# Sixth block pair of a SwiGLU layer in the 11-product Strassen form, with a new order for all engines

## The chip, the cores and the metric

One core of one Trainium2 chip runs the kernel. The metric is the device time of one execution in microseconds (us). Three runs of the kernel before took 2497.64, 2503.82 and 2503.84 us, median 2503.82. The engines are called as the profile calls them: PE is TensorE (PEld its weight load), DVE VectorE, ACT ScalarE, POOL GpSimd, SP the engine that issues most DMAs. Each engine works through its own queue in order and waits on semaphores of the others.

## What is computed

`x` is (8, 4096, 192). Two layers follow each other:

```python
# light convolution: 8 heads of 24 channels, 7 taps, softmax over the taps
w = softmax(weight, axis=-1)
out = einsum('hk,bskhg->bshg', w, windows_of(x_pad, 7))
# SwiGLU feed-forward on the 32768 tokens, d_model 192, d_ff 1536
xn = x / sqrt(mean(x*x, -1) + 1e-6) * rms_g
g = xn @ w_gate
return (silu(g) * (xn @ w_val)) @ w_out
```

## The kernel before, in words

The 32768 tokens are cut into 32 *pairs* of 1024 tokens, a pair being two groups of 512. Pair 0 and the conversion of the weights form the start. Pair 1 is computed with plain f32 matmuls. Pairs 2 to 31 are all computed alike, one *window* of time each.

**Products.** d_ff is 1536 = 12 chunks of 128. Two chunks make a *block pair* j (0 to 5), which together with the two token groups is a 2 x 2 block product with the cells a, b, c, d. Each cell holds the gate (upper half of a PSUM bank pair) and the value (the other). One product of the window (`product`, matmul at L899) is 6 matmuls of 512 columns: three split parts (high, middle, low words of f32, in the type fp32r) by two row halves. In the *plain* form (0 in `FORM`) a block pair takes 12 products, named Aa to Ed. In the *Strassen* form (1) it takes 11, named P1 to P7 and Q1 to Q4, and the cells are put together with copies and sums between the products, which the table `ORDER` names f1, f3, f4 and f5:

```python
if act == "f1":                       # b's bank starts as a copy of a's
    self.open((j, "b"), True)
    copy(eng, self.both(j, "b"), self.both(j, "a"))
elif act == "f3":                     # c's products are put aside in SBUF (tt)
    copy(eng, s5, self.both(j, "c"))
elif act in ("f4", "f5"):             # c = b + s5, later d = b + s5
    c = "c" if act == "f4" else "d"
    ...
    nc.vector.tensor_tensor(out=self.both(j, c), in0=self.both(j, "b"), in1=s5, op=ALU.add)
```

The copies are at L667 (ACT) and L669 (DVE), the sums at L967 (DVE, 128x1024). There are four PSUM bank pairs in all. A cell takes one from its first product until it is evacuated: `g` is the Silu on ACT (L973), `m` the product with the value on DVE (L980), which writes the 128x512 hidden tile `ht` and gives the bank back.

**Out steps.** The second matmul (42 steps a window, `step`, L923, names o1.0 to o7.5) uses a Strassen form as well, with 7 products by 6 block pairs. Step o2.j, for instance, reads a cell that `h2` has overwritten in place, and `h1` to `h4` (`h_sum`, L950, on DVE or POOL) make these sums. h2.j overwrites the cell that step o1.j reads. Steps o1 and o7 open accumulators X and Z, each in a freed bank pair. At the end `c1`, `c2`, `s7` copy accumulators, `C22`, `C21` (L997) add them, `T11` to `T22` (L938) transpose them, and `st` stores them.

**The next pair's input.** While a window runs, other engines prepare the pairs that follow: seven taps of the convolution (`cv0` to `cv6`, L431 and L435, 128x1536), square, reduction, factor and scale (`sq`, `red`, `pow`, `bc`, `mul`), eight DMAs to a scratch tensor in DRAM (`pl`), six DMAs back in the other layout into tile `xb` (`ft`, L631), eight DMAs that load the input of the pair after that (`ld`, L146). Then four sums of token blocks (`x1` to `x4`, `x_sum`, L827; x2 needs x1, x4 needs x2) and the split in three words for each of five operands: `n` is a copy to fp32r (L667 ACT, L669 DVE), `l` and `d` are at L813 and L815.

**Weights.** The split pieces lie in DRAM and are streamed through a ring of 10 slots (`ring<-wd`, L785, 192 KB each, SP). Each freed slot starts the next load; a plain block pair has 6 pieces, a Strassen one 9.

**What sets the order.** Nothing is scheduled at build time: four tables are the order of work. `LINE` is PE's: 69 products and 42 out steps. `ORDER` is one window: each word is an engine letter (V = DVE, G = POOL, A = ACT, S = SP), an act and a block pair or part; `p3` stands for three steps of `LINE`, `-` means the pair before, `+` and `++` the next one and the one after. `FIRST` is the window of pair 1, where `W` is a step of the preparation of the split weights (`prepare`, L749 to L768). `prepare(o)` works on as regular a slice of block pairs as `FORM` allows:

```python
kind = {2: 1, 4: 1, 6: 1, 8: 1, 9: 0}.get(o)
mine = [j for j in range(NP) if kind in (None, FORM[j])]
step = {b - a for a, b in zip(mine, mine[1:])}
if len(step) > 1:
    return slice(0, NP)
```

In `ORDER` of before PE runs, from the window's start, 15 out steps of the pair before, one product, one out step, four products, three out steps, then 64 products without a break and 23 out steps; the long stretches of out steps of two windows join into one of 38.

Of the kernel before, what the change touches and what calls it, by code (L numbers as in the profile page):

```python
# [20 lines left out]
def kernel(  # L21
# [46 lines left out]
    SPAN = 1509  # L68
    SPLIT = 2.0**-12
    HIGH = 0xFFFFF000  # L70
    FORM = (1, 0, 1, 0, 1, 0)
    PLAIN = tuple((j, c) for j in range(NP) for c in "abcd")
    ORDER = (
        "Vd.0 An.4 An.3 Ac2- p5- Gh4.2- Vl.2 Vd.4 Vh4.3- Vl.3 Vd.3 Vl.0 Vd.2 Vh4.0- Vh4.5-",
        "p8- Gh4.4- Gh4.1- VT11- VC22- p2- p1 Gl.4 Acv0+ Af1.0 VT22- VC21- p1- VT21- p3 Vcv1+",
        "p1 Af3.0 Ast1.2- Vcv2+ Vf4.0 p3- p3 Aga.0 Ast1.0- Vcv3+ VT12- Vma.0 Sst0.2- Agc.0",
        "Ast0.3- p1 Vf5.0 p2 Vcv4+ p1 Vmc.0 Vcv5+ p2 Sst1.3- p1 Sst0.4- Sst0.0- Agb.0 Ast1.1-",
        "Agc.1 Ast0.1- Vmb.0 p2 Vcv6+ Agd.0 p2 Aga.1 Vmd.0 Vma.1 Vmc.1 p1 Asq+ Vred+ p1 Af1.2",
        "Sst1.4- Gh1.0 Agb.1 Vmb.1 p1 Gpow+ p3 Af3.2 p1 Vf4.2 p4 Aga.2 Agd.1 Vma.2 Vbc+ Vf5.2",
        "Gmul+ p1 Agc.2 p1 Apl.0+ Apl.1+ Apl.2+ p1 Vmd.1 Vmc.2 p6 Agd.2 Agb.2 Apl.3+ Vmb.2",  # L80
        "Vmd.2 Apl.4+ p1 Agb.3 Aga.3 Apl.5+ p1 Vmb.3 Vma.3 p4 Af1.4 Vf3.4 Agc.3 Apl.6+ Apl.7+",
        "p3 Vmc.3 p1 Vf4.4 p2 Aga.4 Gh1.1 p1 Agd.3 Aft.0+ Sft.2+ Vma.4 Vf5.4 Vh3.1 Sft.3+",
        "Aft.1+ Sld.0++ Vmd.3 Sft.4+ Sld.1++ Sft.5+ Sld.2++ Sld.3++ Sld.4++ Sld.5++ Sld.6++",
        "Sld.7++ p7 Gh1.3 Agc.4 Agd.4 Vmc.4 Vmd.4 Agb.4 p1 Vh1.2 Vh3.0 Vmb.4 p7 An.0+ p1",
        "Aga.5 Agd.5 p1 Vh1.4 An.1+ Vx1+ Vmd.5 Vma.5 p1 Gh3.3 p2 Gh3.2 Agb.5 p2 Gh3.4 p2 Gx3+",
        "Agc.5 Vd.1+ p1 Vh2.0 Vmc.5 Vh2.1 Vmb.5 Vh1.5 Vh2.2 Vh3.5 Vl.1+ Vh2.5 Vh2.4 Ac1 p1",
        "Gx2+ An.2+ p6 Gh2.3 Gx4+ As7 p8",
    )
    FIRST = (
        "p1 Vcv5+ W p2 Vcv6+ p1 Aga.0 Vma.0 p2 Asq+ W W p1 Agb.0 W Vmb.0 W p1 Vred+ p2 Agc.0",  # L90
        "Vmc.0 W p1 Gpow+ W W W p1 W p1 Agd.0 W Vmd.0 p1 Vbc+ Gh1.0 p1 Gmul+ p1 Aga.1 Vh3.0 W",
        "Vma.1 p1 W W W W p1 W p1 Agb.1 Apl.0+ Vmb.1 p1 Apl.1+ p1 Apl.2+ W p1 Agc.1 Apl.3+ W",
        "W W Vmc.1 Apl.4+ p1 W W Apl.5+ p1 Apl.6+ p1 Agd.1 Apl.7+ Vmd.1 p1 Gh1.1 W p1 W W W",
        "p1 Aga.2 Vh3.1 W Vma.2 W p3 Agb.2 Vmb.2 W p1 W W W p1 W p1 Agc.2 W Vmc.2 p3 Agd.2 W",
        "Vmd.2 p1 W W W Vh1.2 W p1 W p1 Aga.3 Gh3.2 Vma.3 p2 W p1 Agb.3 W W W Vmb.3 p1 W W p1",
        "Aft.0+ p1 Aft.1+ Agc.3 Sft.2+ Vmc.3 p1 Sft.3+ W p1 Sft.4+ W W W Sft.5+ p1 Agd.3 W",
        "Vmd.3 W p1 Gh1.3 p2 Aga.4 Gh3.3 Vma.4 W p1 W W p1 W p1 Agb.4 W Vmb.4 p3 Agc.4 W",
        "Vmc.4 p1 W p2 Agd.4 An.1+ Vmd.4 p1 Vx1+ Sld.0++ Vh1.4 p1 Gx3+ Vd.1+ p1 Aga.5 Gh3.4",
        "Vma.5 Vl.1+ Sld.1++ p1 Gx2+ p1 An.2+ p1 Agb.5 Sld.2++ Gx4+ Vmb.5 p1 Sld.3++ p2 Agc.5",
        "Sld.4++ Vmc.5 p1 Sld.5++ p1 Sld.6++ Agd.5 p1 An.0+ Vmd.5 p1 Vh2.0 Sld.7++ Vh1.5 p2",  # L100
        "Gh2.3 Vh3.5 Vh2.5 p1 Vh2.1 p1 Vh2.4 p1 Ac1 Vh2.2 p2 R p7 As7 p7",
    )
    LINE = (
        "P1.0 P5.0 P6.0 P2.0 Q1.0 P7.0 P3.0 Q2.0 Ac.1 Q4.0 Q3.0 P4.0 Bc.1 Ec.1 Aa.1 Ba.1 Ea.1",
        "Ab.1 Eb.1 P1.2 Bb.1 P5.2 P6.2 P2.2 Q1.2 Ad.1 Ed.1 P7.2 P3.2 Bd.1 Q2.2 Q3.2 Q4.2 Aa.3",
        "Ba.3 P4.2 Ea.3 Ab.3 Bb.3 Eb.3 Ac.3 Bc.3 P1.4 P5.4 Ec.3 P6.4 P2.4 Q1.4 Ad.3 Bd.3 P7.4",
        "Ed.3 Q2.4 P3.4 Q4.4 P4.4 Ad.5 Q3.4 Ed.5 Aa.5 Ea.5 Ab.5 Bd.5 Ac.5 Bc.5 Ba.5 Bb.5 Ec.5",
        "Eb.5 o1.0 o1.5 o1.3 o1.1 o1.4 o1.2 o7.0 o7.3 o7.4 o2.0 o7.1 o7.2 o2.5 o6.0 o7.5 o6.2",
        "o2.3 o6.1 o2.4 o6.4 o6.3 o6.5 o4.4 o2.1 o4.1 o5.0 o2.2 o5.5 o4.3 o5.3 o4.5 o5.2 o5.4",
        "o5.1 o4.2 o4.0 o3.5 o3.2 o3.3 o3.1 o3.4 o3.0",  # L110
    )

    cst = ctx.enter_context(tc.tile_pool(name="cst", bufs=1))
# [605 lines left out]
    def blocks(o):  # L719
# [4 lines that stand above are left out]
# [600 lines left out]
```

## Time and profile before

| | |
|---|---|
| three runs | 2497.64, 2503.82, 2503.84 us |
| the profiled execution | 2498.01 us, span 2496.2 us, granted PE clock 0.999 |
| PE busy | 2477.4 us, 29140 matmul records |
| DVE busy | 2013.4 us, 2482 instructions |
| ACT, POOL busy | 926.6 and 852.5 us |
| one window, 373.85 to 449.52 us | 75.67 us: PE 75.67, DVE 62.62, ACT 27.90, POOL 26.14 busy |
| window of pair 1, 129.04 to 222.66 us | 93.62 us: PE 93.62, DVE 67.77, ACT 36.72, POOL 43.72 busy |

Part 1 of the page gives busy time by engine, part 4 the chain of work that ended last (what each step on it waited for), part 5 the costliest groups of instructions by line. The trace also answers with the chain in order of time and with timelines of one engine, in which a bracket tells how long the engine sat idle before an instruction and what ended that.

### The profile page before, as it was taken

What the parts mean: (1) busy time and instruction counts of PE and PEld (TensorE: products, weight loads), DVE (VectorE), ACT (ScalarE), POOL (GpSimd) and SP (SyncE); (2) the same over time, 40 slices, a digit from 0 to 9 for tenths busy, and PEclk for the clock granted to TensorE, in tenths of its full rate; (3) what the DMA queues carried; (4) which work ended last, traced back from release to release, by engine and by line L of the source; (5) the groups of instructions that cost most, each with busy time, mean ns of one, the idle gap of its engine ahead of it and who ended that gap; (6) DMA issues with size and microseconds to landing.
All of it is one profiled execution on the core that took longest, in us unless ns stands there. A gap on an engine that the chain in (4) does not pass through costs nothing.

```text
span 2496.2 us, 69094 instructions
## 1 busy us (share of the span) xinstructions
PE 2477.4 (99%) x29140; PEld 1932.4 (77%) x29140; DVE 2013.4 (81%) x2482; ACT 926.6 (37%) x1349; POOL 852.5 (34%) x640
## 2 busy tenths in 40 slices
PE   8999999999999999999999999999999999999999
PEld 5647778877777787777877788777777877778887
DVE  8668888788878788878888788888787888888864
ACT  6443334333333333333333343333333333333331
POOL 0553333423243324343333333233433233333331
PEclk9999999999999999999999999999999999999999
DMA  7365667766678666677666677666686666786652
GB/s 150 59 189 152 155 170 192 173 180 157 156 171 205 169 166 158 160 180 193 172 160 157 168 192 176 179 154 157 170 201 172 165 158 162 181 197 171 159 140 81
DMA packets 701735, 412.22 MB, mean 165 GB/s; under 512 B 506610, under 2 KB 687730, under 8 KB 701426
## 3 DMA queue, kind: packets, MB, share of 16 engines
q1 hardware_dynamic: 540176, 353.65, 56.1%
q10 hardware_dynamic: 161250, 54.16, 9.7%
q8 instruction: 230, 3.77, 0.6%
q14 instruction: 79, 0.65, 0.1%
HBM read 349.26 MB, written 58.39 MB: 163 GB/s over the span
## 4 chain that ended last, share of the span: by engine, by line
PE 96%; DMA 2%; SPq 1%; DVE 0%; ACT 0%; issue 0%; ACTq 0%; DVEq 0%
PE ps L899 56%; PE ps L923 34%; PE ps L871 2%; PE ps L1070 2%; DMA xb<-xd 1%; PE ps L1111 1%; SPq L146 0%; SPq L229 0%; DMA ht<-in_moe_w_gate_dram 0%; DMA x<-in_x_dram 0%; DMA ht<-in_moe_w_val_dram 0%; ACT tt L973 0%; DVE ht L980 0%; SPq L631 0%; ACT o_sb L1119 0%
## 5 line engine op out<-in xcount | busy, mean ns | idle before, releaser
L899 PE MATMUL ps<-part,ring 64*128 64x512 f32 x12420 | 1442.9, 389 | 0.0
L899 PEld LDWEIGHTS ps<-part,ring 64*128 64x128 f32 x12420 | 1185.8, 184 | 236.5 <-issue 18.0
L973 ACT ACTIVATE tt<-ps 128x512 f32<-128x512 f32 x744 | 430.9, 598 | 726.4 <-PE ps L899 586.4
L980 DVE TENSOR_TENSOR ht<-ps,tt 128x512 f32<-128x512 f32 x744 | 495.5, 684 | 190.5 <-ACT tt L973 185.3
L923 PE MATMUL ps<-ht,wo_sb 128*32 128x384 f32 (+2 forms) x6696 | 443.1, 380 | 3.3 <-DVE ht L980 3.3
L923 PE MATMUL ps<-ht,x 128*32 128x256 f32 (+2 forms) x6696 | 441.9, 379 | 0.0
L950 POOL TENSOR_TENSOR ht<-ht 128x512 f32<-128x512 f32 x186 | 283.7, 1538 | 433.3 <-PE ps L923 377.1
L950 POOL TENSOR_TENSOR hs<-ht 128x512 f32<-128x512 f32 x93 | 120.2, 1293 | 834.2 <-DVE ht L980 832.3
L923 PEld LDWEIGHTS ps<-ht,wo_sb 128*32 128x32 f32 x6696 | 296.2, 110 | 121.9 <-issue 21.5
L923 PEld LDWEIGHTS ps<-ht,x 128*32 128x32 f32 x6696 | 302.5, 110 | 90.6
L435 DVE SCALAR_TENSOR_TENSOR y<-xh,tp,y 128x1536 f32<-128x1536 f32 x186 | 342.5, 1841 | 1.3
L667 ACT COPY ps<-ps 128x384 f32<-128x384 f32 (+1 forms) x121 | 104.1, 860 | 408.7 <-PE ps L899 311.7
L967 DVE TENSOR_TENSOR ps<-ps,tt 128x1024 f32<-128x1024 f32 x180 | 221.3, 1229 | 42.1 <-PE ps L899 35.0
L667 ACT COPY tt<-ps 128x384 f32<-128x384 f32 (+1 forms) x122 | 91.0, 746 | 227.0 <-PE ps L923 207.8
L923 PE MATMUL ps<-hs,x 128*32 128x128 f32 (+2 forms) x2232 | 161.0, 379 | 0.0
L950 DVE TENSOR_TENSOR ht<-ht 128x512 f32<-128x512 f32 x186 | 126.5, 693 | 8.0 <-POOL hs L950 4.6
L923 PEld LDWEIGHTS ps<-hs,x 128*32 128x32 f32 x2232 | 108.9, 110 | 27.7
L667 ACT CAST part<-xb 128x1024 fp32r<-128x1024 f32 x87 | 91.3, 1050 | 104.0 <-DMA xb<-xd 67.1
L950 DVE TENSOR_TENSOR ht<-hs,ht 128x512 f32<-128x512 f32 x155 | 122.4, 806 | 2.9 <-PE ps L923 1.1
L950 DVE TENSOR_TENSOR hs<-ht 128x512 f32<-128x512 f32 x93 | 116.4, 1252 | 2.1
L815 DVE SCALAR_TENSOR_TENSOR part<-part,xb 128x1024 fp32r<-128x1024 f32 x87 | 105.5, 1213 | 0.0
L813 DVE TENSOR_TENSOR part<-xb,part 128x1024 fp32r<-128x1024 f32 x87 | 105.4, 1212 | 0.0
(136 smaller groups left out, 1460.1 us busy)
## 6 DMA issues: line engine op xcount, KB each, us to landing
ring<-wd SPq DMA_DIRECT2D x1350, 192.0 KB
xb<-xd SPq DMA_DIRECT2D x122, 256.0 KB
xd<-xh ACTq DMA_DIRECT2D x240, 96.0 KB
xh<-in_x_dram SPq DMA_DIRECT2D x192, 105.0 KB
xb<-xd ACTq DMA_DIRECT2D x58, 256.0 KB
out_dram<-o_sb ACTq DMA_DIRECT2D x93, 96.0 KB
wd<-part SPq DMA_DIRECT2D x5, 1152.0 KB
xh<-in_x_dram SPq DMA_DIRECT2D x56, 98.4 KB
```

The source lines that it names most:

```text
L435: nc.vector.scalar_tensor_tensor(out=y, in0=xk, scalar=w, in1=y, op0=ALU.mult, op1=ALU.add)
L667: nc.scalar.copy(out=dst, in_=src)
L813: e.tensor_tensor(out=split_of(g, 1).bitcast(F32R), in0=src, in1=high, op=ALU.subtract)
L815: nc.vector.scalar_tensor_tensor(out=split_of(g, 2).bitcast(F32R), in0=high, scalar=1.0 + SPLIT, in1=src, op0=ALU.mult, op1=ALU.subtract,)
L871: nc.tensor.matmul(out=self.both(j, c)[:, h, :], lhsT=wf[HALF[h], k, 2 * j + f, :], rhs=rb[HALF[h], k, g, :], start=(k == 0), stop=(k == K ...
L899: nc.tensor.matmul(out=self.both(j, c)[:, h, :], lhsT=left[HALF[h]], rhs=right[HALF[h]], start=(first and q == 0), stop=True, skip_group_c ...
L923: nc.tensor.matmul(out=self.acc(b)[i * Q : (i + 1) * Q, at : at + n], lhsT=left, rhs=cols, start=fresh, stop=True, skip_group_check=True, ...
L950: engine[eng].tensor_tensor(out=dst, in0=a, in1=b, op=op)
L967: nc.vector.tensor_tensor(out=self.both(j, c), in0=self.both(j, "b"), in1=s5, op=ALU.add)
L973: nc.scalar.activation(out=tt[:, t, :], in_=self.both(j, c)[:, 0, :], func=AF.Silu)
L980: nc.vector.tensor_tensor(out=self.hv(j, "abcd".index(c)), in0=self.both(j, c)[:, 1, :], in1=tt[:, t, :], op=ALU.mult,)
L1070: nc.tensor.matmul(out=bank(h, bks[h])[:], lhsT=wf[HALF[h], AT[h][k], u * NF + f, :], rhs=xb[HALF[h], g, k, :], start=(k == 0), stop=(k == ...
```

## The change

`FORM` sets the sixth block pair to the Strassen form. `ORDER`, `FIRST` and `LINE` are replaced as a whole; the functions stay. The sixth pair's 12 products Aa.5 to Ed.5 become 11 (P1.5 to Q4.5); one each of f1, f3, f4 and f5 is added; the window has 68 products and 110 PE steps. Three of the five copies `n` go from ACT to DVE, all f3 to ACT, `s7` and `x3` to DVE, all h2 to DVE, all eight `pl` from ACT to SP. The kernel's lines move down by 2.

```diff
-    FORM = (1, 0, 1, 0, 1, 0)
+    FORM = (1, 0, 1, 0, 1, 1)
     ORDER = (
-        "Vd.0 An.4 An.3 Ac2- p5- Gh4.2- Vl.2 Vd.4 Vh4.3- Vl.3 Vd.3 Vl.0 Vd.2 Vh4.0- Vh4.5-",
-        "p8- Gh4.4- Gh4.1- VT11- VC22- p2- p1 Gl.4 Acv0+ Af1.0 VT22- VC21- p1- VT21- p3 Vcv1+",
-        "p1 Af3.0 Ast1.2- Vcv2+ Vf4.0 p3- p3 Aga.0 Ast1.0- Vcv3+ VT12- Vma.0 Sst0.2- Agc.0",
...
-        "p3 Vmc.3 p1 Vf4.4 p2 Aga.4 Gh1.1 p1 Agd.3 Aft.0+ Sft.2+ Vma.4 Vf5.4 Vh3.1 Sft.3+",
-        "Aft.1+ Sld.0++ Vmd.3 Sft.4+ Sld.1++ Sft.5+ Sld.2++ Sld.3++ Sld.4++ Sld.5++ Sld.6++",
-        "Sld.7++ p7 Gh1.3 Agc.4 Agd.4 Vmc.4 Vmd.4 Agb.4 p1 Vh1.2 Vh3.0 Vmb.4 p7 An.0+ p1",
-        "Aga.5 Agd.5 p1 Vh1.4 An.1+ Vx1+ Vmd.5 Vma.5 p1 Gh3.3 p2 Gh3.2 Agb.5 p2 Gh3.4 p2 Gx3+",
-        "Agc.5 Vd.1+ p1 Vh2.0 Vmc.5 Vh2.1 Vmb.5 Vh1.5 Vh2.2 Vh3.5 Vl.1+ Vh2.5 Vh2.4 Ac1 p1",
-        "Gx2+ An.2+ p6 Gh2.3 Gx4+ As7 p8",
+        "p3- p2 Ast1.0- Af1.0 Ast1.2- p3- p1 Af3.0 Vf4.0 VT12- p7 Sst0.4- Ast1.1- Aga.0",
...
+        "Agb.2 p2 Af1.4 Vmb.2 Spl.5+ Agc.1 p3 Af3.4 Spl.6+ Vmc.1 Vf4.4 p1 Spl.7+ p6 Agd.1",
+        "Aga.4 Vma.4 Vmd.1 p3 Aft.0+ Agc.4 Vf5.4 Aft.1+ p1 Agb.3 Vmc.4 Vmb.3 Sft.2+ p4 Sft.3+",
+        "Gh1.1 Gh3.0 Gh3.1 Gh1.2 Sld.0++ Sld.1++ Sld.2++ Agd.4 Sld.3++ Sft.4+ Sft.5+ Agb.4",
+        "Sld.4++ Sld.5++ Sld.6++ Sld.7++ Vh1.3 Vmd.4 Af1.5 p1 Vmb.4 p1 Vh3.2 Vn.0+ p2 Af3.5",
+        "p1 Aga.5 p1 Vf4.5 Vma.5 p3 Vf5.5 p3 Vd.0+ Vx1+ Agc.5 Agd.5 Aga.3 Vn.1+ Vmd.5 p1",
+        "Vh2.0 Agb.5 Vmb.5 p3 Gh1.4 Gh3.4 Vma.3 p2 Gl.0+ p4 Gx2+ Gx4+ Vx3+ Vh3.3 Vh1.5 Vh3.5",
+        "Vh2.1 Vh2.5 Vd.1+ Vh2.3 Vh2.2 Vmc.5 Vh2.4 An.3+ Ac1 p7 Vs7 p9 An.2+ Ac2 Gh4.1 p10",
+        "Vn.4+ Gh4.4 Vh4.3 Vl.1+ Vd.3+ Vl.3+ Vd.2+ Vl.4+ Vl.2+ Vd.4+ Gh4.2 VT11 VC22 VT22",
+        "Acv0++ Vh4.0 VC21 Gh4.5 VT21 Vcv1++ Vcv2++ Vcv3++",
...
     LINE = (
-        "P1.0 P5.0 P6.0 P2.0 Q1.0 P7.0 P3.0 Q2.0 Ac.1 Q4.0 Q3.0 P4.0 Bc.1 Ec.1 Aa.1 Ba.1 Ea.1",
...
-        "Ed.3 Q2.4 P3.4 Q4.4 P4.4 Ad.5 Q3.4 Ed.5 Aa.5 Ea.5 Ab.5 Bd.5 Ac.5 Bc.5 Ba.5 Bb.5 Ec.5",
-        "Eb.5 o1.0 o1.5 o1.3 o1.1 o1.4 o1.2 o7.0 o7.3 o7.4 o2.0 o7.1 o7.2 o2.5 o6.0 o7.5 o6.2",
...
+        "P5.0 P1.0 P6.0 P2.0 Q1.0 P3.0 Q2.0 P7.0 Aa.1 Ea.1 Ab.1 Bb.1 Eb.1 P4.0 Q4.0 Q3.0 Ba.1",
...
+        "Q4.4 P4.4 Q3.4 P1.5 Aa.3 Ea.3 P5.5 P6.5 Q1.5 P2.5 Ba.3 P7.5 Q2.5 P3.5 Q4.5 P4.5 Q3.5",
+        "o1.0 o1.2 o1.5 o7.0 o1.1 o1.4 o1.3 o7.1 o7.2 o7.4 o7.5 o2.2 o2.3 o7.3 o6.0 o2.1 o6.5",
...
```

## The prediction, as it was put on record

> **What bounds the kernel now.** I read the page first: busy time (part 1), then the chain that ended last (part 4).
>
> ```profile
> PE 2477.4 (99%) x29140; PEld 1932.4 (77%) x29140; DVE 2013.4 (81%) x2482; ACT 926.6 (37%) x1349; POOL 852.5 (34%) x640
> ...
> PE 96%; DMA 2%; SPq 1%; DVE 0%; ACT 0%; issue 0%; ACTq 0%; DVEq 0%
> ```
>
> PE is busy and it is the chain. So the second view is that chain in order of time, from 222 to 380 us. It gives one window in rows.
>
> ```profile
> 266.69 24.84 PE ps L923 x304
> 291.53 0.91 PE ps L899 x6
> 292.44 0.79 PE ps L923 x8
> 293.22 2.95 PE ps L899 x24
> 296.17 2.09 PE ps L923 x24
> 298.26 44.04 PE ps L899 x384
> ```
>
> Columns are start, length, what. Here are 38 out steps, 1 product, 1 out step, 4 products, 3 out steps, 64 products: 75.62 us without a gap. Over the whole chain the 44-us pieces start 2196.06 us apart over 29 windows (222.66 to 2418.72), 75.73 each; the 0.11 more is a few windows with a late input. A product costs 44.04/64 = 0.688, an out step 24.84/38 = 0.654. The short pieces cost more than that: 0.91 + 2.95 for 5 products (3.44) and 0.79 + 2.09 for 4 out steps (2.61) are 0.69 over, for two excursions from out steps to products and back, 0.34 each.
>
> Third, who could make PE wait: the DVE's timeline in the window of 373.85, around the end of its products.
>
> ```profile
> 375.26 1.23 DVE L967 TENSOR_TENSOR ps<-ps,tt 128x1024 f32<-128x1024 f32 x1
> 376.40 1.81 DVE L435 SCALAR_TENSOR_TENSOR y<-xh,tp,y 128x1536 f32<-128x1536 f32 x1
> ...
> 409.79 1.72 DVE L950 TENSOR_TENSOR hs<-ht 128x512 f32<-128x512 f32 x1
> 411.42 0.68 DVE L950 TENSOR_TENSOR ht<-ht 128x512 f32<-128x512 f32 x1
> 412.03 0.68 DVE L980 TENSOR_TENSOR ht<-ps,tt 128x512 f32<-128x512 f32 x1
> 412.74 1.06 DVE L950 TENSOR_TENSOR hs<-ht 128x512 f32<-128x512 f32 x1
> 415.82 1.14 DVE L827 TENSOR_TENSOR tt<-xb 128x512 f32<-128x512 f32 x1 [2.02 <-DMA xb<-xd]
> 417.10 1.29 DVE L980 TENSOR_TENSOR ht<-ps,tt 128x512 f32<-128x512 f32 x2
> 418.30 1.22 DVE L815 SCALAR_TENSOR_TENSOR part<-part,xb 128x1024 fp32r<-128x1024 f32 x1
> 419.43 0.68 DVE L950 TENSOR_TENSOR ht<-hs,ht 128x512 f32<-128x512 f32 x1
> ```
>
> And POOL's, at the same time:
>
> ```profile
> 409.66 1.29 POOL L950 TENSOR_TENSOR ht<-ht 128x512 f32<-128x512 f32 x1
> 411.58 1.67 POOL L950 TENSOR_TENSOR ht<-ht 128x512 f32<-128x512 f32 x1 [0.63 <-DVE hs L950]
> ```
>
> The same 128x512 sum takes DVE 0.68 or 1.72. At 409.79 POOL had begun 0.13 us before and ended at 410.95; DVE's sum ended at 411.51, 0.56 later. At 412.74 again: POOL's ends at 413.25, DVE's at 413.80, 0.55 later. So a DVE sum of two SBUF tensors waits until a POOL sum that is under way has ended. Where DVE is first (411.42 to 412.10), POOL's (411.58) is the longer one, 1.67, and ends 1.15 after DVE's. A DVE operation with one side in PSUM (L980 at 412.03) takes its 0.68 all the same.
>
> The Trainium skill says the same of a cause, in "GPSIMD Engine Reference", Key points: POOL shares its SBUF interfaces with VectorE and contends with DVE instructions that have two SBUF inputs or run in a 2-port mode. These rows agree for two inputs; none here shows the 2-port case.
>
> **The change, part by part.**
>
> *PE.* The build order has 20600 matmul instructions against 20780: 180 fewer = 30 windows x 6, so the form is what the change says. One product less is 0.69. The new order has out steps (36 + 3), two products (P5.0, P1.0), three out steps, 66 products: one excursion where there were two, 0.34 less. PE's own work is 75.62 - 0.69 - 0.34 = 74.59 a window. If nothing waits, 30 x (75.73 - 74.59 - 0.11) = 31 us go.
>
> *DVE.* Added: f4.5, f5.5 (2 x 1.14 start to start), three n, one h2 (0.6), x3 (0.6), s7 (0.5); gone: one f3 (1.15), one h4 (0.6). For n on DVE the trace has no row. Bounds: below, one 128x512 SBUF copy at L553 took 0.42, against 0.684 for a two-input operation of that size (L980) and 1.212 for 1024 columns (L813); taking the same fixed part (0.156) a copy of 1024 would be 0.69. Above: the 1.21 of L813. I take 0.69, 0.62 start to start, since the copy row is the nearest. DVE's load rises from 62.6 to about 66.7 of 74.6 us. It fits as a sum; it is a matter of place.
>
> The Trainium skill ("VectorE: DVE Perf Modes", The perf-mode tier table) gives f32 copies within SBUF twice the rate, 1227 ns for 2048 elements. That fits the 0.42; with its 1x figure, n would be near the upper bound.
>
> *The switch from products to out steps.* This is the stretch that decides. DVE's new queue there is f5.5, d.0, x1, n.1, m (cell d.5), h2.0, m (b.5). o1.0, the first out step, opens accumulator X in the bank that m of d.5 gives back; o7.0, three steps later, takes that of b.5. f5.5 can't begin before P7.5 has ended, and between that and o1.0 PE has 5 products, 3.44 us. Set P7.5's end to 0. DVE: f5.5 1.14, d.0 1.13 (418.30 to 419.43), x1 0.61, n.1 0.62, m 0.68 to its end: 4.18. o1.0 starts at 4.2 instead of 3.44: **0.8 late**. The cover that before had here was large: its x1 sat 2.02 us waiting for a DMA, and PE lost nothing.
>
> Then h2.0 overwrites what o1.0 reads, so it can't begin before o1.0 has ended, at 4.95. POOL meanwhile: x1 ends at 2.95, x2 follows at 3.03 (POOL starts 0.08 after a DVE end, as at 411.58 after 411.51) and ends at 4.33, and x4, right behind it in POOL's queue, runs till 5.6. If a DVE copy holds POOL up as a DVE sum does (no row shows it either way), x2 ends 1.15 after n.1 (3.57), at 4.72, and x4 at 6.0. In both h2.0 finds POOL busy, ends 0.55 after it (6.15 or 6.55), m of b.5 behind it ends at 6.8 or 7.2, and o7.0, which PE would reach at 3.44 + 3 x 0.65 = 5.40, is **1.4 to 1.8 late** in all (the 0.8 included). I take 1.6. What is queued behind has time: the cells of the next out steps are due after that.
>
> Sum: 74.59 + 1.6 + 0.11 = 76.30 against 75.73, 0.57 more, 30 windows: **+17 us**.
>
> *SP and DMA.* Three more ring loads a window (48 for 45), 0.59 MB, 0.32 us of SP each. Eight pl move from ACT to SP, about 0.6 each as on ACT (392.73, three in 1.95). SP was idle for much of its loads' waits (1089 us in all for PE to free a slot), which hides both; the ring is 10 pieces ahead, some 7 us of products. ACT is freed of its waits on pl (74.7 us in its waits), which hid behind nothing late. Cost 0 either way.
>
> *The first window.* `prepare` now takes all six block pairs for pieces 2, 4, 6, 8: POOL 4 x 0.81 (1812 against 1000 ns at L762) and as much for the differences, some 6 us on top of 43.72 of 93.62; DVE 4 x 0.4. PE's 93.62 hide it; if the last piece came late, the ring's start, nine out steps into the pair's 42, would still have 30 steps. 0. The tail after the last product keeps its 42 steps: 0.
>
> Total: 2498.0 (profiled execution: span 2496.2 and 1.8 around it) + 17 = 2515. The runs are 2497.64, 2503.82, 2503.84, so their median lies 5.8 over the profiled one; I add half: **2518 us**.
>
> **Rivals.** *h2.0 gets the port before x4.* Then only the 0.8 is left: 74.59 + 0.84 + 0.11 = 75.54, 6 us less than before, 2495 with the same 3 added: not slower. It decides at 4.95: x4 must start later than o1.0 ends, that is x2 0.2 to 0.6 later than reckoned, by an earlier POOL sum that runs over. For it: POOL has h1.4, h3.4 and l.0 (2.38) just before. Against: by their inputs these end ahead of x1. *No wait at all.* If the stretch costs PE nothing, as today, 31 us go: 2470. For it: before, the same stretch took 2 us of DMA wait unharmed. Against: that had slack, and the sum of rows is 0.74 over. *The DMA wait moves into DVE's queue.* n.0 and x1 are fed by ft. In before n.0 stood on ACT, which waited 67.1 us for it in 18 windows, up to 5.0. On DVE f4.5 stands behind it, then f5.5 with hardly any slack. 1 us a window more gives 2548. For it: ft now waits for pl at the end of SP's queue. Against: the four ft no longer start together, and land sooner. If n is slow (1.21), DVE alone is 1.3 late, but x4 then ends sooner than in the second case, and o7.0 is again 1.4 late: the main case.
>
> **The numbers.** Main case 0.45 (2512 to 2524, 2518), port taken first 0.17 (2495), no wait 0.15 (2470), DMA in the queue 0.13 (2548), rest, of both signs, 0.10. A measurement here tells 0.3% from no change, 7.5 us around 2503.8. Faster than 2496.3: the no-wait case and over half of the port case, 0.25. Within: the rest of that and the lower end of the main case, 0.17. Slower: 0.58. The range reaches half way to the no-wait case and takes in most of the DMA case: 2482 to 2546. The main case alone: 2511 to 2525.
>
> **What would show it.** In the chain, one excursion a window and 66 products in one piece (right for PE). A PE gap before L923 of 0.8 released by L980, and a second one before o7.0; h2.0 (L950 `ht<-hs,ht`) of 1.2 to 1.7 us beside POOL's L827. Wrong if windows are 74.6 apart, or if the wait stands before products, behind DVE's L669 `part<-xb` with a DMA as releaser. A DVE copy `part<-xb` of 1.2 would show n slow.

## The result, and the profile after

| | before | after |
|---|---|---|
| median of four runs | 2503.32 us | **2693.21 us** (2689.93 to 2701.97) |
| profiled execution | 2498.01, span 2496.2 | 2689.93, span 2688.1 |
| mean distance of windows | 75.73 us | 81.66 us |

The ratio is 1.077, 95% interval 1.074 to 1.080: 190 us slower, where 2518 with 2482 to 2546 was forecast. The profiled execution took 191.9 us more: 29 windows by 5.93 are 172, and the first window is some 18 longer. Part 1 and part 4 of the page after:

```profile
PE 2516.0 (94%) x28960; PEld 1945.8 (72%) x28960; DVE 2115.5 (79%) x2663; ACT 923.7 (34%) x1318; POOL 1060.2 (39%) x610
PE 75%; DMA 11%; DVE 9%; issue 2%; POOL 1%; ACT 1%; SPq 1%; DVEq 0%; ACTq 0%; POOLq 0%
```

PE has 180 matmuls fewer and is still busy for 39 us more. It is no longer the whole chain: of that chain 11% is DMA now and 9% DVE, where it was 2% and 0% before. The same chain in order of time, through one window (start, length, what):

```profile
905.00 17.97 PE ps L901 x158
...
924.36 5.05 DMA xb<-xd
...
929.47 2.44 DMA ring<-wd
...
931.95 2.95 PE ps L901 x11
...
947.90 1.44 DVE ht L952
...
950.08 23.61 PE ps L925 x289
```

Products (L901) run until a fetch `xb<-xd` (`ft.1`) is on the chain; when it has landed a ring load starts, and when that has landed PE goes on. At 947.90 the sum h2.0 stands before an out step, as the prediction had it. What a fetch has to do with a ring load is seen in the timeline of SP's own queue (its rows are issues; landings come later), with the waits of SP and of PE in the whole run (us in total, times, longest) behind it:

```profile
921.87 0.54 SPq L1035 DMA_DIRECT2D xd<-xh  x1
922.51 0.56 SPq L787 DMA_DIRECT2D ring<-wd  x1
926.70 0.55 SPq L1035 DMA_DIRECT2D xd<-xh  x1
929.47 2.69 SPq L787 DMA_DIRECT2D ring<-wd  x6
```
```profile
SPq L1035 <- DMA xb<-xd: 112.7, 29, 4.8
...
SPq L787 <- DMA xb<-xd: 25.1, 32, 2.2
```
```profile
PE ps L901 <- DMA ring<-wd: 92.4, 40, 4.2
PE ps L925 <- DVE ht L982: 44.5, 59, 1.2
```

L1035 is `pl`, L787 the ring load. Once in each window a store `pl` waits until a fetch has landed, and the ring loads stand behind it in the same queue. SP issues no ring load in the 6.4 us from 923.1 to 929.5, then six in 2.7 us: six slots stood free by then.

Why a store waits for a fetch is seen in the program as built: each DMA of any engine takes one of eight completion semaphores in turn, and may not start before the DMA that had it before, eight earlier in program order, has landed. ft.0 and ft.1 need only the first four stores, and the program as built has them, on ACT, between pl.3 and pl.4, though `ORDER` names them behind pl.7 (the table fixes each engine's own queue, not this count). So the last `pl` (SP) stands eight behind ft.0 (ACT), and the ring load after it eight behind ft.1. In this window ft.0 was issued at 923.13 and the held `pl` at 926.70; ft.1 was issued at 924.36 and had landed at 929.41, just before the ring load.

The three ring loads more a window were not too much for the DMA engines in this window: in the stretch where PE ran dry they had little to do. Views of single stretches (start:end, length, busy of PE, PEld, DVE, ACT, POOL with counts, granted PE clock, DMA share, GB/s):

```profile
926.70:929.50 2.80, 1.01 (x10) 0.50 (x6) 1.92 (x4) 1.20 (x2) 2.80 (x3) 1.00 0.30 69
```
```profile
936.00:937.00 1.00, 1.00 (x8) 0.80 (x6) 1.00 (x3) 0.80 (x1) 0.68 (x1) 0.50 1.01 262
938.00:940.00 2.00, 2.00 (x20) 1.66 (x18) 0.53 (x1) 0.77 (x1) 1.95 (x2) 0.97 0.75 195
```

The DMA share is 0.30 in the first. The other two show what the pause costs beyond itself: from 932 to 938 PE's granted clock was 0.50, and products came 1.28 us apart instead of 0.68.

In nine of the windows PE waited for a slow transfer too: the ring load issued just ahead of the held `pl` took 4.3 to 5.3 us to land beside the fetches, where a ring load behind the hold took 2.3 to 2.8 (in one of them from 1088.17 to 1093.44, with a DMA share of 0.73 in its last 2.6 us). These waits are 18 of the 110 us for which PE's weight loads wait for the ring.

What each PE step takes too long, from its start to the next one's and as a mean of 29 windows, adds up as follows. The six products from Bb.3 to P1.5 take 4.5 us more than they should (Q4.4 alone 2.8), some 1.1 of it by the halved clock; o1.0 comes 0.64 late and o7.0 another 1.18. With the 74.59 of the prediction this leaves 0.75 of the 81.66 for small waits elsewhere, most before Q4.5 and at Q1.0.

### The profile page after: what moved, and what is told of

Its sections match the earlier page's. It is cut to its first block, busy times and chain, and to the rows that moved or that the text cites. A ratio compares the mean times of both kernels' runs of the same rounds, so it can differ in the third digit from the quotient of the medians.

```text
span 2688.1 us, 69112 instructions
## 1 busy us (share of the span) xinstructions
PE 2516.0 (94%) x28960; PEld 1945.8 (72%) x28960; DVE 2115.5 (79%) x2663; ACT 923.7 (34%) x1318; POOL 1060.2 (39%) x610
## 4 chain that ended last, share of the span: by engine, by line
PE 75%; DMA 11%; DVE 9%; issue 2%; POOL 1%; ACT 1%; SPq 1%; DVEq 0%; ACTq 0%; POOLq 0%
PE ps L901 43%; PE ps L925 30%; DMA xb<-xd 4%; DMA ring<-wd 4%; DVE ht L982 2%; DVE ht L952 2%; DVE part L817 1%; DMA xd<-xh 1%; DVE part L671 1%; PE ps L1113 1%; DVE tt L829 1%; ACT tt L975 1%; DMA wd<-part 1%; DVE y L437 0%; SPq L148 0%
## 5 line engine op out<-in xcount | busy, mean ns | idle before, releaser
L901 PE MATMUL ps<-part,ring 64*128 64x512 f32 x12240 | 1471.0, 396 | 97.0 <-DMA ring<-wd 92.4
L901 PEld LDWEIGHTS ps<-part,ring 64*128 64x128 f32 x12240 | 1177.6, 188 | 376.7 <-DMA ring<-wd 110.4
L952 POOL TENSOR_TENSOR ht<-ht 128x512 f32<-128x512 f32 x217 | 545.8, 2534 | 337.2 <-PE ps L925 334.1
L925 PE MATMUL ps<-ht,x 128*32 128x256 f32 (+2 forms) x6696 | 414.6, 380 | 38.5 <-DVE ht L982 28.7
L969 DVE TENSOR_TENSOR ps<-ps,tt 128x1024 f32<-128x1024 f32 x240 | 295.9, 1233 | 99.1 <-ACT tt L669 65.7
L669 ACT COPY ps<-ps 128x1024 f32<-128x1024 f32 (+1 forms) x151 | 134.6, 892 | 457.6 <-PE ps L901 303.4
L669 ACT COPY tt<-ps 128x1024 f32<-128x1024 f32 (+1 forms) x151 | 137.1, 908 | 364.5 <-PE ps L925 289.8
L952 DVE TENSOR_TENSOR ht<-hs,ht 128x512 f32<-128x512 f32 x186 | 145.3, 809 | 30.3 <-PE ps L925 30.2
L952 DVE TENSOR_TENSOR ht<-ht 128x512 f32<-128x512 f32 x155 | 105.6, 681 | 9.3 <-PE ps L925 8.2
L487 POOL TENSOR_TENSOR xh<-y,s 128x1536 f32<-128x1536 f32 x30 | 90.4, 3014 | 12.8 <-DVE s L479 9.0
L940 DVE STREAM_TRANSPOSE o_sb<-ps 128x256 f32<-128x256 f32 x124 | 39.8, 360 | 47.6 <-PE ps L925 37.6
```

Of the source, the lines that this page charges most:

```text
L487: e.tensor_tensor(out=yn[p].rearrange("p a t -> p t a"), in0=y, in1=ss[:].rearrange("p (t o) -> p t o", o=1).to_broadcast([P, TB, GS]), op ...
L669: nc.scalar.copy(out=dst, in_=src)
L901: nc.tensor.matmul(out=self.both(j, c)[:, h, :], lhsT=left[HALF[h]], rhs=right[HALF[h]], start=(first and q == 0), stop=True, skip_group_c ...
L925: nc.tensor.matmul(out=self.acc(b)[i * Q : (i + 1) * Q, at : at + n], lhsT=left, rhs=cols, start=fresh, stop=True, skip_group_check=True, ...
L940: nc.vector.transpose(out=to[:, n, lo:hi], in_=src[:, lo * Q : hi * Q].rearrange("p (b e) -> p b e", e=Q),)
L952: engine[eng].tensor_tensor(out=dst, in0=a, in1=b, op=op)
```

## The experiments

All are edits of the changed kernel or of one another, but for the eighth. Times are medians of four runs; the ratio is to runs of the kernel before on the same chip.

| | us | ratio, 95% interval | mean window |
|---|---|---|---|
| changed kernel | 2693.2 | 1.077 (1.074 to 1.080) | 81.66 |
| e1_pl_act | 2627.5 | 1.050 (1.048 to 1.053) | 79.50 |
| e2_ft_sp | 2614.2 | 1.045 (1.044 to 1.047) | 79.26 |
| e3_b5_first | 2604.0 | 1.042 (1.039 to 1.044) | 78.53 |
| e4_d5_first | 2631.7 | 1.052 (1.050 to 1.054) | 79.66 |
| e5_f1_first | 2579.9 | 1.032 (1.030 to 1.034) | 77.79 |
| e6_d5_b5 | 2598.0 | 1.040 (1.038 to 1.042) | 78.48 |
| e7_first | 2605.8 | 1.042 (1.041 to 1.044) | 78.63 |
| e8_before_pl_sp (old form) | 2580.8 | 1.032 (1.031 to 1.034) | 78.55, before 75.73 |
| e9_spread | 2558.0 | 1.023 (1.021 to 1.025) | 77.10 |
| e10_pool | 2639.8 | 1.055 (1.054 to 1.057) | 79.92 |
| e11_prep | 2552.9 | 1.021 (1.019 to 1.023) | 77.40 |
| e12_words | 2544.8 | 1.018 (1.017 to 1.020) | 77.07 |

**Is it SP's queue?** First the stores back on ACT:

```diff
-Spl.0+ ... Spl.7+      (ORDER)
+Apl.0+ ... Apl.7+
```

> One edit to the changed kernel: in ORDER (windows 2 to 31) the eight pl, which store the squared and scaled tokens, are issued by ACT again, as before the change; FIRST is left as it is. Queue theory: in the changed kernel PE waits for ring pieces 110.4 us at its weight loads (44 times), because the last pl stands in SP's queue until ft.0, which ACT issues, has landed (SP waits 112.7 us for xb<-xd at the pl's line, 29 times), and the ring loads stand behind it. With pl on ACT, SP's queue holds no wait on ft.0 ahead of ring loads: the ring waits go, some 4.6 us in each of 30 windows, 138 us, so 2692 - 138 = 2554 us (2535 to 2570), the page's wait of PE for ring<-wd falls under 20 us, and 55 us of switch stalls (1.82 a window) and 18 of the first window stay. Rival, transfers: the three more ring loads a window are too much for the DMA engines or for ten slots; then the ring waits stay, 2680 to 2700.

PE's ring waits fell from 92.4 to 2.5 us, as the queue theory had it, and not a transfer was taken away: the rival, that the transfers by themselves are too many, is out. But the time fell by 66 us, not 138. PE got a new wait, 45.5 us in 30 times, for ACT. ACT's queue and PE in one window:

```profile
1212.05 3.68 ACTq L1035 DMA_DIRECT2D xd<-xh  x5
1215.83 0.60 ACT L975 ACTIVATE tt<-ps 128x512 f32<-128x512 f32 x1 [3.26 <-DMA xd<-xh]
...
1216.32 1.02 ACT L669 COPY ps<-ps 128x1024 f32<-128x1024 f32 x1
```
```profile
1217.39 2.79 PE L901 MATMUL ps<-part,ring 64*128 64x512 f32 x22 [1.44 <-ACT ps L669]
```

Five issues of `pl` in a row hold ACT for 3.7 us, and the copy f1.4 that P6.4 needs stands behind them: 1.7 us a window. The new order had been made with these eight off ACT.

```diff
-Aft.0+ Aft.1+      (ORDER)
+Sft.0+ Sft.1+
```

> One edit to the changed kernel: in ORDER ft.0 and ft.1, which fetch the tokens back, are issued by SP instead of ACT; the eight pl stay on SP. All loads and stores of this part are then in one queue, ft.0 behind the last pl in it, so that no pl waits for a fetch. Queue theory: the hold of 4 to 6 us goes, what stays is ft.0's own wait for the last stores to land (2 to 3 us from issue), with some ring loads ahead of it: ring waits of 0 to 2 us a window, 2555 to 2615 us. Rival, pl on SP is enough: SP stands at pl.0 until POOL has made the scaled tokens, and eight issues of 0.6 us take 5 us from it; then it is no better here, 2680 to 2700. Rival, transfers: 2680 to 2700.

With the eight stores left on SP and the two fetches put behind them in the same queue, no `pl` waits for a fetch. The 4.5 us fell to 0.2 at the old place (Bb.3 to P1.5), and 2614 is at the edge of what was expected. The hold was the pairing with a fetch on another queue; SP's own time to issue eight `pl` costs little.

But 1.5 us came back at Q1.5 to Ba.3, and not for the reason that was expected: ft.0 stood on SP for the last stores 0.36 us at most. Here the transfers are slow. SP's rows and PE's in one window, and the stretch in which PE stood:

```profile
985.38 1.14 SPq L633 DMA_DIRECT2D xb<-xd  x2
986.62 0.53 SPq L787 DMA_DIRECT2D ring<-wd  x1
```
```profile
993.70 6.36 PE L901 MATMUL ps<-part,ring 64*128 64x512 f32 x48 [1.59 <-DMA ring<-wd]
```
```profile
992.00:993.70 1.70, 0.11 (x4) 0.01 (x2) 0.89 (x2) 0.00 (x0) 0.88 (x2) 1.00 1.02 182
```

The ring load issued right behind the first two fetches landed after 7.0 us, and the DMA share was 1.02 while PE waited. In all 29 places from pair 2 on where PE's weight loads waited over 0.8 us for the ring, the load had taken 4.1 to 7.9 us. So in this run the rival has a share: the ring load has to share the DMA engines with the fetches of 256 KB just ahead of it. Nothing was run that spreads them.

The same move alone, in the kernel before:

```diff
-Apl.0+ ... Apl.7+      (ORDER of the kernel before)
+Spl.0+ ... Spl.7+
```

> The kernel before with one edit: in ORDER the eight pl are issued by SP instead of ACT, nothing else. Queue theory: SP's queue now holds the pl and, behind them, ring loads that wait until the fetches ft.0 and ft.1 have landed, so ring loads stop for some us and PE waits for ring<-wd: 2 to 5 us a window, 2560 to 2650 us, in a kernel that has the old form, 45 ring loads and the old order. Rival, the new form's transfers: the move costs nothing by itself, 2495 to 2510.

It cost 81 us, 2.8 a window, in the old form with its 45 loads. Part 4 of its page and one line each of SP's and PE's waits:

```profile
PE 86%; DMA 11%; SPq 1%; issue 1%; ACTq 0%; DVE 0%; ACT 0%; DVEq 0%
```
```profile
SPq L785 <- DMA xb<-xd: 193.7, 62, 6.4
```
```profile
PE ps L899 <- DMA ring<-wd: 38.5, 43, 2.0
```

DMA's share of the chain is the 11% of the changed kernel. Ring waits are only a part of it: the fetches come later too, DVE's wait for them at x1 grew from 54.2 to 154.0 us, and 15.7 us of PE's waits are for DVE's products behind that x1. The two make 54 of the 81 us; the rest was not told apart.

**The switch to the out steps.** On top of e1:

```diff
-Vh2.0 Agb.5 Vmb.5
+Agb.5 Vmb.5 Vh2.0
```

> pl on ACT as in the first kernel of this call, and in ORDER the product of cell b.5 (Agb.5 Vmb.5) ahead of Vh2.0, so that the bank for o7.0 is given back before DVE's sum h2.0 waits for o1.0's end and for POOL's x2 and x4. Prediction's theory: o7.0 comes 1.18 us late a window in the changed kernel for that wait; with the edit that goes, 30 x 1.2 = 35 us below the first kernel (25 to 40). Rival, DVE is late as a whole: m of b.5 is late because the queue before it is, h2.0's wait is only where it shows; then the gain is under 10 us, and o1.0's stall grows or stays with o7.0's.

The step ahead of o7.0 went from 1.82 to 0.645, its own time: 1.17 a window, so the wait was what h2.0's place made it. The window fell by 0.97 only, since 0.26 came back at Q1.0 and 0.19 before P6.4, and the run by 23 us, just under the 25 to 40 expected.

```diff
-Vd.0+ Vx1+ Agc.5 Agd.5 Aga.3 Vn.1+ Vmd.5 p1 Agb.5 Vmb.5
+Agc.5 Agd.5 Aga.3 Vmd.5 Vd.0+ Vx1+ Vn.1+ p1 Agb.5 Vmb.5
```

> As the third kernel, and in ORDER d.0, x1 and n.1 behind the product of cell d.5 (Agc.5 Agd.5 Aga.3 Vmd.5 Vd.0 Vx1 Vn.1), so that DVE gives back o1.0's bank 2.4 us sooner. Prediction's theory: o1.0's stall, 0.64 us a window, goes: 30 x 0.64 = 19 us below the third kernel (10 to 22). Then PE has its 74.6 us a window but for what ring waits are left: 2692 - 138 - 35 - 19 = 2500 (2480 to 2515), of which 18 us or so are still in the first window. Rival: the stall goes elsewhere, since d.0, x1 and n.1 and with them POOL's x2 and x4 and DVE's x3 are 0.7 to 2 us later and meet DVE's next sums: 0 to 8 us gained.

The product ahead of o1.0 took 0.96 for 1.47, and o7.0's wait came back with 1.07: the three operations now stood ahead of b.5's product. 28 us slower than e3. The rival was right that the stall goes elsewhere, in the first place that one would look, but it still had 0 to 8 us gained.

```diff
-Apl.3+ Apl.4+ Agb.2 p2 Af1.4 Vmb.2 Apl.5+
+Agb.2 p2 Af1.4 Vmb.2 Apl.3+ Apl.4+ Apl.5+      (on e3)
```

> As the third kernel (pl on ACT, cell b.5 ahead of h2.0), and in ORDER pl.3 and pl.4 behind f1.4 instead of ahead of it. With pl on ACT, PE waits for ACT's f1.4 in every window (45.5 us in 30 waits, before P6.4), which stood behind a row of five pl issues of some 0.6 us each. Queue theory: two of them fewer ahead of f1.4 take 1.2 to 1.9 of the 1.88 us lost there, 36 to 51 us in all: 2604 - 45 = 2559 (2550 to 2570), and no ring wait comes back. Rival, ACT's wait is for the pl's own lane (a pl may not start before an earlier transfer has landed), not for the time of issue: less than 20 us.

24 us for the expected 45. The 1.6 before P6.4 went, and 1.2 appeared before Ad.1, which waits for the bank that the silu of c.1 holds up, now behind three `pl`.

```diff
-Vd.0+ Vx1+ Agc.5 Agd.5 Aga.3 Vn.1+ Vmd.5 p1 Agb.5 Vmb.5 Vh2.0 p3 Gh1.4 Gh3.4 Vma.3
+Vd.0+ Agc.5 Agd.5 Aga.3 Vmd.5 Vx1+ p1 Agb.5 Vmb.5 Vn.1+ Vh2.0 p3 Gh1.4 Gh3.4 Vma.3
```

> As the first kernel of this call, and on DVE at the switch: f5.5, d.0, product of d.5, x1, product of b.5, n.1, h2.0 (there f5.5, d.0, x1, n.1, product of d.5, product of b.5, h2.0). In the fourth kernel of the call before, d.0, x1 and n.1 stood between the two products: o1.0's stall fell by 0.5 us a window, and o7.0's came back with 1.07. Prediction's theory of a DVE that is late at these two banks alone: both stalls are short now, 30 x 0.7 to 0.8 = 21 to 24 us below the first kernel. Rival, DVE is full from here to the end of the window, so that n.1, d, l moved back cost PE as much at Q1.0 or at the first products of the next window: within 8 us of the first kernel.

18 us slower than e5. o1.0's wait fell by 0.47, and a new one of 0.91 came before o1.3, which needs a.3's product, behind n.1 and h2.0 in the queue. Both theories missed that.

The last of this line spreads the `pl` one by one and puts a.3's product ahead of n.1:

```diff
+Vmb.2 Apl.3+ Agc.1 p1 Apl.4+ p1 Apl.5+ p1 Af3.4 Apl.6+
...
+Vd.0+ Agc.5 Agd.5 Aga.3 Vmd.5 Vx1+ p1 Agb.5 Vmb.5 Vma.3 Vn.1+ Vh2.0
```

> The changed kernel with pl on ACT, now one pl ahead of each of several products: pl.3 behind f1.4, pl.4 and pl.5 behind the silu of c.1; at the switch f5.5, d.0, product of d.5, x1, product of b.5, product of a.3, n.1, h2.0. With pl.3 to pl.5 behind f1.4 but ahead of the silu of c.1 the stall had only moved: PE lost 1.2 us a window before Ad.1 for the bank that this silu holds up, and with n.1 ahead of a.3's product 0.9 us before o1.3. Queue theory (each wait is what stands ahead in one queue): both go, and o1.0's stall falls by 0.5: 2580 - 30 x (1.2 + 0.2 + 0.5) = 2523 (2515 to 2540). Rival, ACT and DVE have too little time left in these windows, and whatever is moved is late elsewhere: 2570 to 2600.

2558 lies between the two expectations: both named waits went (Ad.1 0.68, o1.3 0.645), o1.0's fell by 0.47 as before, and 0.29 came back at Q1.0, 0.37 at o7.4, 0.2 at P2.4. A window is still 2.5 us above 74.59, now in some eight small waits. DVE has 67.7 us of work in a 77-us window of this order (66.7 was reckoned), so it is not full as a sum; it is late in places.

```diff
-Gx2+ Gx4+ Vx3+ ... Vh4.3 Vl.1+      (on e9)
+Gx2+ Gx4+ Gx3+ Gl.1+ ... Vh4.3
```

> As the first kernel of this call, and x3 and l.1 on POOL instead of DVE (POOL is idle for 8.8 us of the window there). If DVE's total between the switch and Q1.0 is what makes PE wait 0.4 to 0.7 us at Q1.0, 1.7 us less of it take that away: 10 to 20 us less than the first kernel. Rival, by the rows of both kernels a sum of two SBUF tensors on POOL and one on DVE hold each other up (four POOL sums took 14.5 us beside DVE's l and d): then l.1 on POOL comes late and DVE's sums wait behind POOL's: no gain or up to 60 us more.

Q1.0's wait went, as the first theory said (1.43 to 0.87), and the window grew by 2.8 all the same: 82 us, in the way that the rival said, and more than its 60. PE, then DVE and POOL at one such place:

```profile
1253.81 0.86 PE L925 MATMUL ps<-ht,x 128*32 128x384 f32 x12 [2.77 <-DVE ht L952]
```
```profile
1248.51 1.76 DVE L952 TENSOR_TENSOR ht<-ht 128x512 f32<-128x512 f32 x1
```
```profile
1248.00 1.73 POOL L829 TENSOR_TENSOR tt<-xb 128x512 f32<-128x512 f32 x1
1249.69 2.80 POOL L815 TENSOR_TENSOR part<-xb,part 128x1024 fp32r<-128x1024 f32 x1
```

DVE's sums of 0.68 take 1.76 and, at 1250.20, 2.84 while POOL's x3 and l.1 run: 1.8 us moved off DVE cost it more than they took.

**The first window.** Three runs. On e6, eight operand splits put behind the h sums; on e9, the old size of `prepare`; on e9, the eight splits behind s7:

```diff
-Vl.1+ ... Vd.3+ ... Vl.3+ ... Vd.2+ ... Vd.0+ ... Vl.4+ ... Vl.2+ ... Vd.4+      (FIRST)
+R Vd.0+ Vl.1+ Vd.3+ Vl.3+ Vd.2+ Vl.4+ Vl.2+ Vd.4+      (e7: behind the ring's start)
+Vs7 p2 Gh4.1 Vd.0+ Vl.1+ Vd.3+ Vl.3+ Vd.2+ Vl.4+ Vl.2+ Vd.4+      (e12: behind s7)
```

> As the second kernel of this call, and in FIRST (the window of pair 1) eight operand splits (d.0, l.1, d.3, l.3, d.2, l.4, l.2, d.4) behind the h sums and the ring's start instead of ahead of them. In the changed kernel's first window PE waits 9.8 us once for DVE's ht of L952 before the out steps; eight splits of 1.14 stand ahead of it in DVE's queue. If these are the cause, 8 to 10 us go; if POOL's and DVE's work in prepare of six block pairs is, the wait stays and the time is within 3 us of the second kernel.

The wait did not go, it moved: from 9.8 us before an out step that needs h2 to 9.5 before one that needs s7 (releaser DVE `tt L671`), behind the same eight splits. The time was 8 us above e6, but their intervals overlap, so it can't be told from no change.

```diff
-mine = [j for j in range(NP) if kind in (None, FORM[j])]
+mine = [j for j in range(NP) if kind in (None, (1, 0, 1, 0, 1, 0)[j])]
...
-r = (j * NW + o) * P
+r = ((4 if j == 5 and o in (2, 4, 6, 8) else j) * NW + o) * P
```

> As the first kernel of this call, but prepare makes pieces 2, 4, 6, 8 for three block pairs as in the kernel before, and piece 9 for the other three; block pair 5's loads of these four pieces read block pair 4's. That leaves out block pair 5's own pieces, so the output is not the reference's; all instructions after prepare are the same. If the larger prepare (POOL 1.8 us for 1.0 an operation, four of its transfers twice the size) is why the first window is 18 us longer, most of it goes: 10 to 18 us less than the first kernel. If it is the twelve operand splits in DVE's queue there, within 4 us of it.

Pair 1's 288 matmuls ran without a gap, as in the kernel before; in the changed kernel they came in five pieces. The first lines of PE's timelines, e11 and changed kernel:

```profile
129.12 62.07 PE L873 MATMUL ps<-xb,part 64*128 64x512 f32 x288 [0.72 <-DVE o_sb L1125]
```
```profile
128.59 32.87 PE L873 MATMUL ps<-xb,part 64*128 64x512 f32 x144 [0.72 <-DVE o_sb L1125]
```

The next window began 4.4 us sooner than in e9 (226.5 for 230.9). So the larger prepare is worth 4.4 of the 18 us; which of its engines makes them was not told apart. The whole run was 5 us shorter, between the two expectations, and its interval overlaps that of e9.

> As the spread kernel, and in FIRST the eight operand splits (d.0, l.1, d.3, l.3, d.2, l.4, l.2, d.4) behind the copy s7 that opens the last part of pair 1's out steps. Set right ahead of s7, they had only moved PE's wait of 9.8 us to 9.5 before s7's reader; behind s7 DVE was idle for 7.1 and 2.7 us, waiting for PE. If DVE's queue is all there is to the first window's second wait, it goes: 8 to 10 us less than the spread kernel, 2548 to 2550 against 2558. If the splits are then too late for the first products of the next window, or POOL's sums h4 stand behind DVE's, half of it comes back: 2553 to 2558.

The 9.8-us wait is gone; the next window began at 222.3, 8.6 sooner than in e9, and the run was 13 us shorter, where 8 to 10 were expected. If the two add, splits and prepare are 13 of the 18 us; nearly 2 more had gone with e9's other edits (its next window began 1.8 sooner than the changed kernel's), and the rest was not traced.

No version beat the kernel before: the best is 1.8% slower.

## Why the prediction was wrong, step by step

*PE's own work: right as far as it shows.* 180 matmul records fewer, products at 0.68 to 0.69 wherever the clock was full. No window reached 74.59; the best mean was 77.07.

*n on DVE at 0.69: right where nothing holds it up.* The open point, whether a DVE copy and a POOL sum hold each other up, came out as yes. DVE and POOL at the switch of the changed kernel:

```profile
936.76 1.77 DVE L671 CAST part<-xb 128x1024 fp32r<-128x1024 f32 x1
...
945.60 0.69 DVE L671 CAST part<-xb 128x1024 fp32r<-128x1024 f32 x1
...
947.90 1.44 DVE L952 TENSOR_TENSOR ht<-hs,ht 128x512 f32<-128x512 f32 x1 [1.01 <-PE ps L925]
```
```profile
936.32 1.65 POOL L952 TENSOR_TENSOR hs<-ht 128x512 f32<-128x512 f32 x1 [5.74 <-DVE ht L982]
...
945.77 1.65 POOL L829 TENSOR_TENSOR tt<-tt,xb 128x512 f32<-128x512 f32 x1 [3.71 <-DVE tt L829]
```

The copy at 936.76, begun 0.44 after a POOL sum, took 1.77 and ended 0.56 after it. And n.1 at 945.60, begun first, let POOL's x2 (945.77) end only at 947.42, 1.13 after n.1. Of the two cases that the prediction worked through, this is the later one. n.0 met POOL so in every window and took 1.77 to 1.79; n.1 took 0.69 in every one. By the Trainium skill, "GPSIMD Engine Reference", Key points, POOL contends with DVE instructions that have two SBUF inputs or run in a 2-port mode; here a copy with one input is held up as well, which the page allows for by the mode.

*The switch: right in its mechanism, and in size as a sum.* Forecast: o1.0 0.8 late, o7.0 later still, 1.4 to 1.8 in all. Measured 0.64 and 1.18, 1.82 together, so the first part was a little less and the second more than reckoned. h2.0 at 947.90 waited for x4 (POOL, 947.50 to 948.79) and ended 0.55 after it. e3 took the second part away by the one edit that the working names. By itself this is 1.82 for 1.6, some 6 us over the forecast.

*"SP and DMA ... Cost 0 either way": the step that failed.* It counted SP's time to issue (eight pl by 0.6 us, hidden in its waits for PE) and ACT's freed waits. It did not ask what the moved instruction itself waits for, and what is queued behind it on its new engine. The pl had waited on ACT too, 74.7 us in all, and nothing urgent stood behind them there; on SP every ring load does. 4.5 us a window, some 130 of the 190 us, come at this place, some 32 of these through the halved clock; the 18 us of slow ring loads are in it as well. The cover was "the ring is 10 pieces ahead, some 7 us of products"; the hold of 6.4 us and 2.4 for the next load to land exceed it. The kernel before with this move alone shows the step without the rest of the change.

The rival of a DMA wait had the right queue ("ft now waits for pl at the end of SP's queue"), but sent the wait to DVE, 1 us a window, and not to the loads behind it. Its sign that the wait stands before products was seen; the releaser was the ring.

*"The first window: 0": wrong by 18 us.* PE's 93.62 us did not hide the larger prepare, and it was not the only new work: the eight splits in DVE's queue ahead of the h sums were not counted at all. By e12 and e11 they are 8.6 of the 18, prepare 4.4.

*The sum.* 2515 without the median's correction, 29 x 0.22 = 6 for the switch, 29 x 4.5 = 131 for the ring, 29 x 0.75 = 22 for small waits and 18 for the first window make 2692; the profiled execution took 2689.93. The sign came out right by a term that is a tenth of the loss; as to the other nine tenths, it is luck.

## What to carry to other kernels

When an instruction moves to another queue, write down everything that it may wait for there, completion semaphores included, and then what stands behind it: the cost is the slack of those, not the time to issue it. A queue that feeds the bound engine should hold nothing that waits for another engine's transfer. In a finished order most moves only moved a wait (e4, e5, e6, e7, e10); what lies behind the moved instruction has to be listed before, not only what it is meant to free.

## What was not expected of the hardware

PE's granted clock fell to 0.50 after some of its pauses, and made the loss larger than the pause. In the changed kernel, from pair 2 on, all 17 pauses of 2.73 us or more between products were followed by products at half the rate; of 19 between 1.39 and 2.72 only two were (2.05 and 2.31). In e8 there were six such stretches with no single pause over 1.97.

The length of one pause does not decide it. In e10 PE stood 2.77 to 2.79 us in each of 29 windows; 12 of these pauses were followed by a stretch at 0.50 and 17 were not. The traces' record of the granted clock shows what does: from pair 2 on, all such stretches begin on a fixed grid of 3.41 us and last one cell of it (once two). What counts is how long PE was idle in the cell before. In e10 that was 2.07 us or more before the 12 and 2.03 or less in all other cells; in the changed kernel 1.99 or more before its 19, and 1.85 or less elsewhere. In e1, e3, e4 and e8 the border lies between 1.63 and 1.84. So a pause that falls across two cells can leave the clock as it is, and several short ones in one cell can halve it.

From pair 2 on the clock stood at 0.50 for 68 us in 19 stretches in the changed kernel, for 17 us in five in e1, and never in e12 and in the kernel before. Half of that is lost, some 34 us in the changed kernel. Counted by pairs of matmuls that start 0.43 apart instead of 0.227 it is 32; that count gives 6 in e12, where the clock never fell, so it takes in some short waits too. The Trainium skill, "TensorE: Matmul & The Clock Gate", Part 1, has the clock at half after an idle window of about 3.4 us, and at full again after as long a busy one: the half agrees with the rows (0.50), but 17 of the changed kernel's 19 pauses before such a stretch were shorter than 3.4 us.

Four POOL sums h4, one behind the other, took 14.03 us (958.83) in the changed kernel while DVE ran l and d without a break, each on two SBUF tensors; in e9 three took 5.05, of which only the first 0.97 fell beside an l or d. POOL's mean for these sums was 2534 ns, 1538 before. No wait of PE hung on it.
